# Weights of 48 columns, receptances scaled from PSUM, rows by ScalarE, deeper loads and two units ahead of a branch, in an RWKV attention with balanced experts

## The chip, the cores and the metric

One core of one Trainium2 chip. The metric is the device time of one execution in microseconds (us); quoted times are medians of the runs of one kernel, with lowest and highest. A profile is of one execution; its span is some 2 us less than that execution's time.

## The reference

```python
def attention(r, k, v, w, u):                  # r, k, v: (4, 8, 768, 48)
    state = zeros(B, H, D, D)
    for t in range(S):
        cur = outer(u * k[t], v[t])
        y[t] = r[t] @ (state + cur)
        state = w[:, None] * state + outer(k[t], v[t])     # w in 0.85..0.95

def experts(x, w_gate, w1, w2):                # x: (3072, 384), 8 experts, F = 1024
    # tokens are given to experts greedily by logit, 384 to each
    for e in range(8):
        out[mask[e]] = relu(x[mask[e]] @ w1[e]) @ w2[e]
```

All of it is float32. The output of the attention, (batch, position, head and column), is x.

## The kernel before

The attention is cut into 24 units (4 batches, 6 chunks of 128 positions). Within a chunk k is divided and r multiplied by powers of w, so that the pairs of positions are plain matmuls; this holds only if all w lie in a range, so a flag read at run time chooses between two arms of a branch, `attention_mild` (taken here) and `attention_any`. What is made ahead of the branch lies in the constructor of a class, the units in the arm. This is the constructor's loading, and one unit (HP is 4 pairs of heads, T 128 positions, D 48 columns of a head, DX all 384; tiles named _ps lie in PSUM, into which the matmuls write, the others in SBUF; `bufs` is the number of slots that a tile's name gets in a pool):

```python
self.lpool = ctx.enter_context(tc.tile_pool(name="m_load", bufs=5))       # ahead of the branch
...
for n in range(1, 3):
    self.load(n)            # a tile of lpool for k, one for r; v has fixed tiles
...
self.holds = nc.values_load(flag[0:1, 0:1])                               # the branch
...
def scale(n):                                                             # in the arm
    load(n + 3)
    kt, rt, vt = loaded.pop(n)
    ks, rs = kss[n % 4], rss[n % 2]
    nc.vector.tensor_mul(ks[:, :, 0:D], heads(kt), heads(wk))
    nc.vector.tensor_mul(rs[:, :, 0:D], heads(rt), heads(wr))
    rk = pool.tile([128, DX], F32, name="rk")
    nc.gpsimd.tensor_mul(rk, rt, kt)
    nc.gpsimd.tensor_mul(rk, rk, u_bc)
    dd = pool.tile([128, H], F32, name="dd")
    nc.vector.tensor_reduce(out=dd, in_=heads(rk), axis=AX.X, op=ALU.add)
    AT = pool.tile([128, 2, HP, T], F32, name="AT", bufs=3)
    for h in range(H):                                    # a diagonal for each head
        nc.scalar.activation(AT[:, h % 2, h // 2, :], ident, AF.Copy, scale=dd[:, h:h + 1])
def turn(n):
    ...                                                   # transposes of ks and rs
    kT = pool.tile([128, HP, T], F32, name="kT")          # bufs=2
    nc.scalar.copy(kT, kT_ps)
    rT = pool.tile([128, HP, T], F32, name="rT", bufs=3)
    nc.scalar.copy(rT, rT_ps)
def pairs(n):
    ...                                                   # g_ps = kT x rT, per head
    nc.vector.copy_predicated(out=AT[:, q], mask=..., data=g_ps[:, q])
def outputs(n):
    ...                                                   # y_ps = state x rT + vt x AT
    xT = pool.tile([128, HP, T], F32, name="xT", bufs=6)
    nc.scalar.copy(xT, y_ps)                              # frees y_ps, one buffer
    ...                                                   # kv_ps = ks x vt, to the state
for n in range(N):
    scale(n + 2); turn(n + 1); pairs(n + 1); outputs(n); rows(n - 1)   # shortened
```

The order of instructions on each engine is not that of the source: the compiler deals it from a model of the times, and puts a wait in front of an instruction where it reads or overwrites what another engine has not finished.

## Time and profile before

| | before |
|---|---|
| time, us | 474.58 (473.85 to 474.7), 3 runs |
| start, to g_ps of unit 0 | 23.6 us |
| 24 units | 133.7 us |
| assignment | 22.7 us |
| experts | 288.7 us |

The two views below are of the kernel before: first the waits in the units (engine, line and tile waiting; what for; us in all, times, the longest), then ScalarE's part of the timeline (start, duration, engine, line, operation, tiles, count, and in brackets the idle time ahead of it and what ended it).

```profile
ACT xT L492 <- PE y_ps L489: 34.2, 13, 3.8
```

### The profile page before, as it was taken

The numbers are of one execution on the slowest core, as the hardware profiler recorded it, in microseconds if no ns is written. First come the engines' busy times: TensorE is split into PE (matmuls) and PEld (weight loads), VectorE is DVE, ScalarE is ACT, GpSimd is POOL, SyncE is SP. The second block draws the span as 40 slices with busy tenths as digits, with TensorE's granted clock in tenths as the row PEclk, the third lists the DMA queues.
The fourth block names the chain that finished last, engine by engine and source line by source line (L and its number), as shares of the span: only waits on it lengthen the run. The fifth ranks groups of instructions, "written<-read, shape, count | busy, mean of one in ns | idle before, by whom it ended". The sixth has DMA issues, their size and how long they took to land. (4 is left out here: it accounts for less than half of the span.)

```text
span 468.7 us, 7836 instructions
## 1 busy us (share of the span) xinstructions
PE 409.7 (87%) x2900; PEld 276.4 (59%) x2900; DVE 217.5 (46%) x702; ACT 153.5 (33%) x390; POOL 123.5 (26%) x166
## 2 busy tenths in 40 slices
PE   0499999999999411999999999999999999999994
PEld 0387888889888300556556556556556556556552
DVE  5668878899984475440470460460550630300000
ACT  3668666667674000221221121211211211212200
POOL 2734474556560002021103012012021021301001
PEclk9999999999999855699999999999999999999998
DMA  9747555766631106253017027036035048601000
GB/s 156 114 96 162 125 129 120 156 147 141 139 84 36 58 1 242 79 211 127 34 42 298 31 78 277 18 105 250 17 138 216 17 172 317 203 0 38 13 17 34
DMA packets 93959, 54.36 MB, mean 116 GB/s; under 512 B 77137, under 2 KB 88530, under 8 KB 93906
## 3 DMA queue, kind: packets, MB, share of 16 engines
q1 hardware_dynamic: 89858, 44.05, 34.4%
q0 software_dynamic: 3072, 9.44, 5.5%
q8 instruction: 27, 0.44, 0.4%
q10 hardware_dynamic: 976, 0.21, 0.4%
q14 instruction: 26, 0.21, 0.2%
HBM read 44.25 MB, written 9.44 MB: 115 GB/s over the span
## 5 line engine op out<-in xcount | busy, mean ns | idle before, releaser
L1074 PE MATMUL h_ps<-xT,w 128*128 128x384 f32 x384 | 136.8, 504 | 1.4 <-ACT xT L1066 0.5
L1081 PE MATMUL o_ps<-w,hid 128*128 128x384 f32 x384 | 127.5, 486 | 0.0
L1081 PEld LDWEIGHTS o_ps<-w,hid 128*128 128x128 f32 x384 | 71.9, 190 | 47.2
L1074 PEld LDWEIGHTS h_ps<-xT,w 128*128 128x128 f32 x384 | 69.1, 193 | 45.5 <-issue 10.0
L1075 ACT ACTIVATE hid<-h_ps 128x384 f32<-128x384 f32 x64 | 31.4, 491 | 109.2 <-PE h_ps L1074 107.5
L1055 POOL DMA_INDIRECT xg<-x_rows,tok x24 | 23.3, 970 | 150.1 <-PE h_ps L1074 63.9
L444 ACT ACTIVATE AT<-ident,dd 128x128 f32<-128x128 f32 x192 | 58.8, 392 | 2.4 <-DVE dd L441 2.4
L1084 POOL DMA_INDIRECT out_dram<-o_sb,tok x24 | 23.7, 987 | 127.7 <-ACT o_sb L1083 122.5
L718 DVE TENSOR_TENSOR own<-counts,same 128x64 f32<-128x64 f32 x21 | 4.7, 225 | 102.0 <-PE counts L730 102.0
L1083 ACT COPY o_sb<-o_ps 128x384 f32<-128x384 f32 x24 | 11.5, 479 | 108.3 <-PE o_ps L1081 87.9
L438 POOL TENSOR_TENSOR rk<-rt,kt 128x384 f32<-128x384 f32 x24 | 26.2, 1095 | 41.7 <-DMA rt<-in_r_dram 38.6
L469 PE MATMUL g_ps<-rT,kT 48*128 48x128 f32 x384 | 28.8, 291 | 8.7 <-ACT rT L459 6.5
L472 DVE COPY_PREDICATED AT<-mask,g_ps 128x512 f32<-128x512 uint8 x48 | 32.2, 723 | 6.2 <-PE g_ps L469 6.1
L469 PEld LDWEIGHTS g_ps<-rT,kT 48*128 48x128 f32 x384 | 24.2, 193 | 12.7 <-ACT rT L459 10.2
L489 PE MATMUL y_ps<-AT,vt 128*64 128x128 f32 x384 | 29.7, 275 | 0.2 <-issue 0.2
L439 POOL TENSOR_TENSOR rk<-rk,u_bc 128x384 f32<-128x384 f32 x24 | 26.1, 1089 | 1.6
L492 ACT COPY xT<-y_ps 128x512 f32<-128x512 f32 x24 | 14.1, 586 | 36.9 <-PE y_ps L489 34.2
L485 PE MATMUL y_ps<-rT,state 128*64 128x128 f32 x320 | 25.7, 282 | 0.0
L489 PEld LDWEIGHTS y_ps<-AT,vt 128*64 128x64 f32 x384 | 24.6, 137 | 1.3 <-issue 0.4
L435 DVE TENSOR_TENSOR rs<-rt,wr 128x384 f32<-128x384 f32 x24 | 23.9, 996 | 0.7 <-ACT wr L361 0.2
L1066 ACT COPY xT<-xT_ps 128x384 f32<-128x384 f32 x24 | 10.9, 486 | 35.6 <-PE counts L730 32.0
L507 POOL TENSOR_TENSOR state<-state,wp 64x192 f32<-64x192 f32 x32 | 18.7, 584 | 11.2 <-DVE state L506 10.0
(170 smaller groups left out, 431.0 us busy)
## 6 DMA issues: line engine op xcount, KB each, us to landing
w<-in_moe_w_dram SPq DMA_DIRECT2D x16, 1536.0 KB, 8.0
kt<-in_k_dram SPq DMA_DIRECT2D x24, 192.0 KB, 3.6
rt<-in_r_dram SPq DMA_DIRECT2D x24, 192.0 KB, 3.3
vt<-in_v_dram SPq DMA_DIRECT2D x24, 192.0 KB, 3.6
x_rows<-xt SPq DMA_DIRECT2D x24, 192.0 KB, 2.3
xg<-x_rows,tok POOLq DMA_INDIRECT x24, 6.3
out_dram<-o_sb,tok POOLq DMA_INDIRECT x24, 2.6
u_bc<-in_u_dram ACTq DMA_DIRECT2D x1, 192.0 KB, 3.7
```

The source lines that it names most:

```text
L435: nc.vector.tensor_mul(rs[:, :, 0:D], heads(rt), heads(wr))
L438: nc.gpsimd.tensor_mul(rk, rt, kt)
L439: marks["rk"] = nc.gpsimd.tensor_mul(rk, rk, u_bc).ins
L444: nc.scalar.activation(AT[:, h % 2, h // 2, :], ident, AF.Copy, scale=dd[:, h:h + 1])
L469: g = nc.tensor.matmul(g_ps[:, q, a, :], kT[rows, a, :], rT[rows, a, :], start=True, stop=True)
L472: marks["AT"] = nc.vector.copy_predicated(out=AT[:, q], mask=mask.unsqueeze(1).to_broadcast([128, HP, T]), data=g_ps[:, q]).ins
L485: nc.tensor.matmul(y_ps[halves[q], a, :], S0[:, a, q, :], rT[:, a, :], start=(a == 0), stop=False, skip_group_check=True)
L489: nc.tensor.matmul(y_ps[halves[q], a, :], vt[:, 2 * a + q, :], AT[:, q, a, :], start=(c == 0 and a == 0), stop=(a == HP - 1), skip_group_c ...
L1074: nc.tensor.matmul(h_ps, w1[:, f, ts(j, 128)], xT[:, f, :], start=(f == 0), stop=(f == KD - 1))
L1075: nc.scalar.activation(hid[:, j, :], h_ps, AF.Relu)
L1081: nc.tensor.matmul(o_ps, hid[:, j, ts(c, 128)], w2[:, j, :], start=(j == 0), stop=(j == KF - 1))
L1084: nc.gpsimd.indirect_dma_start(out=out_rows[n * NC + c], out_offset=bass.IndirectOffsetOnAxis(ap=tok[:, c:c + 1], axis=0), in_=o_sb, in_of ...
```

## The change

Its intent: less for TensorE to load, a scaled copy of r saved, work moved off VectorE, and the first two units made while the flag is still on its way. The core of the diff, with cuts:

```diff
+        self.pool = ctx.enter_context(tc.tile_pool(name="m_work", bufs=2))     # ahead of the branch
-        self.lpool = ctx.enter_context(tc.tile_pool(name="m_load", bufs=5))
...                     # the transfer of w stands first; rt gets fixed tiles
+            (... for n in (("vt", 8), ("rt", 6), ("ks", 4)))
-        for n in range(1, 3):
+        for n in range(1, 4):
             self.load(n)
...
+            self.scale(0)
+            self.turn(0, ps)
+            self.scale(1)                                # still ahead of the branch
...
+        kt = self.pool.tile([128, H, D], F32, name="kt", bufs=6)
...                     # scale and turn become methods, with tiles of self.pool
+        AT = pool.tile([128, 2, H // 2, T], F32, name="AT", bufs=3)
+        rT = pool.tile([128, HP, T], F32, name="rT", bufs=3)
+        nc.vector.tensor_mul(rT, rT_ps, self.wr)
+        kT = pool.tile([128, HP, T], F32, name="kT")
+        nc.scalar.copy(kT, kT_ps)
...
-                nc.tensor.matmul(y_ps[halves[q], a, :], vt[:, 2 * a + q, :], AT[:, q, a, :],
+                nc.tensor.matmul(y_ps[halves[q], a, :], vt[:, 2 * a + q, 0:D], AT[:, q, a, :],
...                     # 48 columns for state and ks likewise; y_ps zeroed once
-        nc.vector.tensor_copy(heads(xt), xr_ps...)
+        nc.scalar.copy(xt..., xr_ps...)
...
-    scale(0)
-    scale(1)
-    turn(0)
     pairs(0)
```

More of the change, by code (lines that the diff above doesn't have):

```diff
@@ L24, with attention_any @@
 W_MIN, W_MAX = 0.7, 1.2
-def attention_any(ctx, tc, r, k, v, w, u, wg, x_dram, LG, ident, walk):
+def attention_any(ctx, kpads, rpads, tc, r, k, v, w, u, wg, x_dram, LG, ident, walk):
     nc = tc.nc
@@ L48, in attention_any @@
     ps_y = ctx.enter_context(tc.tile_pool(name="a_ps_y", bufs=1, space=PSUM))
-    NB = 3
-    kpads = [const.tile([128, H, PD], F32, name=f"kpad{i}") for i in range(NB)]
-    rpads = [const.tile([128, H, PD], F32, name=f"rpad{i}") for i in range(NB)]
+    NB = len(kpads)
     for i in range(NB):
@@ L293, in __init__ @@
         L = M + 1
-        self.tc, self.sources = tc, (k, r, v)
+        self.tc, self.r, self.k, self.v, self.ident = tc, r, k, v, ident
         const = self.const = ctx.enter_context(tc.tile_pool(name="m_const", bufs=1))
-        self.lpool = ctx.enter_context(tc.tile_pool(name="m_load", bufs=5))
+        self.pool = ctx.enter_context(tc.tile_pool(name="m_work", bufs=2))
         self.units = [(b, c) for c in range(C) for b in range(B)]
-        self.loaded = {}
-        self.vts, self.kss, self.rss = (
-            [const.tile([128, H, PD], F32, name=f"{name}{i}") for i in range(n)]
-            for name, n in (("vt", 6), ("ks", 4), ("rs", 2)))
-        for t in self.vts + self.kss + self.rss:
-            nc.vector.memset(t[:, :, D:PD], 0.0)
-        mask = const.tile([128, 128], F32, name="mask_f")
-        make_upper_triangular(nc, mask, val=1.0, diag=False)
-        self.mask = const.tile([128, 128], U8, name="mask")
-        nc.gpsimd.tensor_copy(self.mask, mask)
-        self.state = [const.tile([128, HP, 2, PD], F32, name=f"state{b}") for b in range(B)]
-        for t in self.state:
-            nc.scalar.activation(t.rearrange("p a q d -> p a (q d)"),
-                                 ident.unsqueeze(1).to_broadcast([128, HP, 128]), AF.Copy, scale=0.0)
-        self.wg_sb = const.tile([128, HP, 32], F32, name="wg_sb")
-        nc.vector.memset(self.wg_sb, 0.0)
+        self.loaded, self.live, self.marks = {}, {}, {}
         flat = w.rearrange("h d -> (h d)")
+        row = const.tile([1, DX], F32, name="row")
         wp = const.tile([P2, 8, HP], F32, name="wp")
@@ L321, in __init__ @@
                 nc.scalar.dma_start(wp[q * PD:q * PD + D, 0, :], w.rearrange("(a q) d -> q d a", q=2)[q])
-        row = const.tile([1, DX], F32, name="row")
         nc.sync.dma_start(row, flat.unsqueeze(0))
+        self.vts, self.rts, self.kss = (
+            [const.tile([128, H, PD], F32, name=f"{name}{i}") for i in range(n)]
+            for name, n in (("vt", 8), ("rt", 6), ("ks", 4)))
+        for i in range(8):
+            for t in (self.rts, self.vts, self.kss):
+                if i < len(t):
+                    (nc.vector if i < 2 else nc.gpsimd).memset(t[i][:, :, D:PD], 0.0)
+        self.wg_sb = const.tile([128, HP, 32], F32, name="wg_sb")
+        nc.vector.memset(self.wg_sb, 0.0)
         self.u_bc = const.tile([128, DX], F32, name="u_bc")
@@ L326, in __init__ @@
         nc.scalar.dma_start(self.u_bc, u.rearrange("h d -> (h d)").partition_broadcast(128))
+        for n in range(1, 4):
+            self.load(n)
         for q in range(2):
@@ L329, in __init__ @@
                                 wg.rearrange("(a q d) e -> q d a e", q=2, d=D)[q])
-        for n in range(1, 3):
-            self.load(n)
         up = const.tile([P2, HP, M + 2], F32, name="up")
@@ L350, in __init__ @@
         nc.vector.reciprocal(ch[:, :, L:T + 2], up[:, :, 1:M + 2])
-        turned = const.tile([P2, HP, T], F32, name="turned")
-        nc.scalar.copy(turned, ch[:, :, T + 1:1:-1])
-        self.wp, self.scales = wp, []
-        with tc.tile_pool(name="m_ps", bufs=2, space=PSUM) as ps, ExitStack() as part:
-            for name, t in (("wk", ch), ("wr", turned)):
-                sc_ps = ps.tile([128, HP, P2], F32, name="sc_ps")
-                for a in range(HP):
-                    nc.tensor.transpose(sc_ps[:, a, :], t[:, a, 0:T], ident[0:P2, 0:P2])
-                sc = const.tile([128, DX], F32, name=name)
-                nc.scalar.copy(sc.rearrange("p (h d) -> p h d", h=H),
-                               sc_ps.rearrange("p a (q d) -> p (a q) d", q=2)[:, :, 0:D])
-                self.scales.append(sc)
+        self.wr = const.tile([P2, HP, T], F32, name="wr")
+        nc.scalar.copy(self.wr, ch[:, :, T + 1:1:-1])
+        self.wp = wp
+        mask = const.tile([128, 128], F32, name="mask_f")
+        make_upper_triangular(nc, mask, val=1.0, diag=False)
+        self.mask = const.tile([128, 128], U8, name="mask")
+        nc.gpsimd.tensor_copy(self.mask, mask)
+        self.state = [const.tile([128, HP, 2, PD], F32, name=f"state{b}") for b in range(B)]
+        for t in self.state:
+            nc.scalar.activation(t.rearrange("p a q d -> p a (q d)"),
+                                 ident.unsqueeze(1).to_broadcast([128, HP, 128]), AF.Copy, scale=0.0)
+        with tc.tile_pool(name="m_ps", bufs=1, space=PSUM) as ps, ExitStack() as part:
+            sc_ps = ps.tile([128, HP, P2], F32, name="sc_ps")
+            for a in range(HP):
+                nc.tensor.transpose(sc_ps[:, a, :], ch[:, a, 0:T], ident)
+            self.wk = const.tile([128, DX], F32, name="wk")
+            nc.scalar.copy(self.wk.rearrange("p (h d) -> p h d", h=H),
+                           sc_ps.rearrange("p a (q d) -> p (a q) d", q=2)[:, :, 0:D])
+            self.scale(0)
+            self.turn(0, ps)
+            self.scale(1)
             pool = part.enter_context(tc.tile_pool(name="mild", bufs=1))
@@ L377, in load @@
         b, c = self.units[n]
-        tiles = []
-        for name, src in zip(("kt", "rt", "vt"), self.sources):
-            H, D = src.shape[1], src.shape[3]
-            if name == "vt":
-                t = self.vts[n % len(self.vts)]
-                into = t[:, :, 0:D]
-            else:
-                t = self.lpool.tile([128, H * D], F32, name=name)
-                into = t.rearrange("p (h d) -> p h d", h=H)
-            self.tc.nc.sync.dma_start(into, src[b, :, ts(c, T), :].rearrange("h s d -> s h d"))
-            tiles.append(t)
@@ L389, in load, with scale @@
-        self.loaded[n] = tiles
+        H, D = self.r.shape[1], self.r.shape[3]
+        kt = self.pool.tile([128, H, D], F32, name="kt", bufs=6)
+        rt, vt = (ts_[n % len(ts_)] for ts_ in (self.rts, self.vts))
+        for src, into in ((self.k, kt), (self.r, rt[:, :, 0:D]), (self.v, vt[:, :, 0:D])):
+            self.tc.nc.sync.dma_start(into, src[b, :, ts(c, T), :].rearrange("h s d -> s h d"))
+        self.loaded[n] = kt, rt, vt
+    def scale(self, n):
+        nc, pool = self.tc.nc, self.pool
+        H, D = self.r.shape[1], self.r.shape[3]
+        self.load(n + 4)
+        kt, rt, vt = self.loaded.pop(n)
+        ks = self.kss[n % len(self.kss)]
+        nc.vector.tensor_mul(ks[:, :, 0:D], kt, self.wk.rearrange("p (h d) -> p h d", h=H))
+        rk = pool.tile([128, H, D], F32, name="rk")
+        nc.gpsimd.tensor_mul(rk, rt[:, :, 0:D], kt)
+        self.marks["rk"] = nc.gpsimd.tensor_mul(rk, rk, self.u_bc.rearrange("p (h d) -> p h d", h=H)).ins
+        dd = pool.tile([128, H], F32, name="dd")
+        nc.vector.tensor_reduce(out=dd, in_=rk, axis=AX.X, op=ALU.add)
+        AT = pool.tile([128, 2, H // 2, T], F32, name="AT", bufs=3)
+        for h in range(H):
+            nc.scalar.activation(AT[:, h % 2, h // 2, :], self.ident, AF.Copy, scale=dd[:, h:h + 1])
+        self.live[n] = dict(vt=vt, ks=ks, rt=rt, AT=AT)
@@ new lines, in turn @@
+    def turn(self, n, ps):
+        nc, pool = self.tc.nc, self.pool
+        HP = self.r.shape[1] // 2
+        ks, rt = self.live[n]["ks"], self.live[n].pop("rt")
+        rT_ps = ps.tile([128, HP, T], F32, name="rT_ps")
+        for a in range(HP):
+            nc.tensor.transpose(rT_ps[:, a, :], rt[:, 2 * a:2 * a + 2, :].rearrange("p q d -> p (q d)"), self.ident)
+        kT_ps = ps.tile([128, HP, T], F32, name="kT_ps")
+        for a in range(HP):
+            nc.tensor.transpose(kT_ps[:, a, :], ks[:, 2 * a:2 * a + 2, :].rearrange("p q d -> p (q d)"), self.ident)
+        rT = pool.tile([128, HP, T], F32, name="rT", bufs=3)
+        nc.vector.tensor_mul(rT, rT_ps, self.wr)
+        kT = pool.tile([128, HP, T], F32, name="kT")
+        nc.scalar.copy(kT, kT_ps)
+        self.live[n].update(kT=kT, rT=rT)
@@ L410, in attention_mild @@
     E = wg.shape[1]
-    const = ctx.enter_context(tc.tile_pool(name="a_const", bufs=1))
     pool = ctx.enter_context(tc.tile_pool(name="a_work", bufs=2))
     ps = ctx.enter_context(tc.tile_pool(name="a_ps", bufs=1, space=PSUM))
-    units, load, loaded = mild.units, mild.load, mild.loaded
-    u_bc, wg_sb, wp = mild.u_bc, mild.wg_sb, mild.wp
-    wk, wr = mild.scales
-    halves = [slice(q * PD, q * PD + PD) for q in range(2)]
-    kss, rss, mask, state = mild.kss, mild.rss, mild.mask, mild.state
-    live, turned, marks = {}, {}, {}
-    def heads(t):
-        return t.rearrange("p (h d) -> p h d", h=H)
-    def pair(t, a):
-        return t[:, 2 * a:2 * a + 2, :].rearrange("p q d -> p (q d)")
-    def scale(n):
-        load(n + 3)
-        kt, rt, vt = loaded.pop(n)
-        ks, rs = kss[n % 4], rss[n % 2]
-        nc.vector.tensor_mul(ks[:, :, 0:D], heads(kt), heads(wk))
-        nc.vector.tensor_mul(rs[:, :, 0:D], heads(rt), heads(wr))
-        rk = pool.tile([128, DX], F32, name="rk")
-        nc.gpsimd.tensor_mul(rk, rt, kt)
-        marks["rk"] = nc.gpsimd.tensor_mul(rk, rk, u_bc).ins
-        dd = pool.tile([128, H], F32, name="dd")
-        nc.vector.tensor_reduce(out=dd, in_=heads(rk), axis=AX.X, op=ALU.add)
-        AT = pool.tile([128, 2, HP, T], F32, name="AT", bufs=3)
-        for h in range(H):
-            nc.scalar.activation(AT[:, h % 2, h // 2, :], ident, AF.Copy, scale=dd[:, h:h + 1])
-        live[n] = dict(vt=vt, ks=ks, rs=rs, AT=AT)
-    def turn(n):
-        ks, rs = live[n]["ks"], live[n]["rs"]
-        kT_ps = ps.tile([128, HP, T], F32, name="kT_ps")
-        for a in range(HP):
-            nc.tensor.transpose(kT_ps[:, a, :], pair(ks, a), ident)
-        rT_ps = ps.tile([128, HP, T], F32, name="rT_ps")
-        for a in range(HP):
-            nc.tensor.transpose(rT_ps[:, a, :], pair(rs, a), ident)
-        kT = pool.tile([128, HP, T], F32, name="kT")
-        nc.scalar.copy(kT, kT_ps)
-        rT = pool.tile([128, HP, T], F32, name="rT", bufs=3)
-        nc.scalar.copy(rT, rT_ps)
-        live[n].update(kT=kT, rT=rT)
+    units, live, marks = mild.units, mild.live, mild.marks
+    wg_sb, wp, mask, state = mild.wg_sb, mild.wp, mild.mask, mild.state
+    halves = [slice(q * PD, q * PD + D) for q in range(2)]
+    y_ps = ps.tile([128, HP, T], F32, name="y_ps")
+    nc.vector.memset(y_ps, 0.0)
+    turned = {}
     def pairs(n):
@@ L467, in pairs @@
             for q in range(2):
-                rows = slice(q * PD, q * PD + D)
-                g = nc.tensor.matmul(g_ps[:, q, a, :], kT[rows, a, :], rT[rows, a, :], start=True, stop=True)
+                g = nc.tensor.matmul(g_ps[:, q, a, :], kT[halves[q], a, :], rT[halves[q], a, :], start=True, stop=True)
         live[n].update(g=g.ins)
@@ L480, in outputs @@
         S0 = state[b]
-        y_ps = ps.tile([128, HP, T], F32, name="y_ps")
         if c > 0:
@@ L484, in outputs @@
                 for q in range(2):
-                    nc.tensor.matmul(y_ps[halves[q], a, :], S0[:, a, q, :], rT[:, a, :],
+                    nc.tensor.matmul(y_ps[halves[q], a, :], S0[:, a, q, 0:D], rT[:, a, :],
                                      start=(a == 0), stop=False, skip_group_check=True)
@@ L499, in outputs @@
                     for q in range(2):
-                        nc.tensor.matmul(kv_ps[halves[q], a, :], ks[:, 2 * a + q, :], vt[:, 2 * a + q, 0:D],
+                        nc.tensor.matmul(kv_ps[halves[q], a, :], ks[:, 2 * a + q, 0:D], vt[:, 2 * a + q, 0:D],
                                          start=True, stop=True)
@@ L503, in outputs @@
                 own = S0[halves[q], :, q, 0:D]
-                wc = wp[halves[q], 7, :].unsqueeze(2).to_broadcast([PD, HP, D])
+                wc = wp[halves[q], 7, :].unsqueeze(2).to_broadcast([D, HP, D])
                 if c > 0:
@@ L517, in rows @@
         xt = pool.tile([128, DX], F32, name="xt", bufs=3)
-        nc.vector.tensor_copy(heads(xt), xr_ps.rearrange("p a (q d) -> p (a q) d", q=2)[:, :, 0:D])
+        nc.scalar.copy(xt.rearrange("p (h d) -> p h d", h=H),
+                       xr_ps.rearrange("p a (q d) -> p (a q) d", q=2)[:, :, 0:D])
         nc.sync.dma_start(x_dram[ts(b * C + c, 128), :], xt)
@@ L541, in attention_mild @@
         if n + 2 < N:
-            scale(n + 2)
+            mild.scale(n + 2)
         if n + 1 < N:
-            turn(n + 1)
+            mild.turn(n + 1, ps)
             pairs(n + 1)
@@ L1027, in rwkv5_eagle_then_base_layer_balanced @@
             with ExitStack() as arm:
-                attention_any(arm, *arguments)
+                attention_any(arm, mild.kss[0:3], mild.rts[0:3], *arguments)
     walk.open(ctx)
```

## The prediction

> **What bounds the kernel now.** I read the stretches first, to know which part the change can reach at all.
>
> ```profile
> core 0: us, PE busy (x) PEld busy (x) DVE busy (x) ACT busy (x) POOL busy (x), PEclk, DMA share, GB/s
> 23.60:157.30 133.70, 130.82 (x1884) 114.12 (x1884) 104.86 (x211) 89.48 (x252) 64.17 (x94) 1.00 0.54 120
> 157.30:180.00 22.70, 2.96 (x24) 1.56 (x25) 15.87 (x73) 0.00 (x0) 0.00 (x0) 0.60 0.05 14
> 180.00:468.70 288.70, 270.95 (x972) 156.86 (x971) 81.78 (x376) 53.07 (x112) 46.96 (x48) 0.97 0.34 121
> ```
>
> The program is a start of 23.6 us, the 24 attention units in 133.7 us (5.57 each), an assignment of 22.7 us on VectorE, and the experts, 288.7 us. The diff touches the first two stretches: 157.3 us of the 468.7 us span. In the units TensorE is busy for 130.8 of 133.7 us; VectorE (104.9) and ScalarE (89.5) have room. So the units are TensorE's, if its busy time is real work; and the start is a chain. The start, from the timeline:
>
> ```profile
> 3.17 0.95 ACTq L321 DMA_DIRECT2D wp<-in_w_dram  x2
> 7.39 0.17 DVE L337 TENSOR_SCALAR wp<-wp 128x4 f32<-128x4 f32 x1 [3.20 <-DMA wp<-in_w_dram]
> 9.66 1.78 DVE L350 RECIPROCAL ch<-up 128x260 f32<-128x260 f32 x1
> 13.56 0.48 ACT L361 COPY wr<-sc_ps 128x384 f32<-128x384 f32 x1 [0.37 <-PE sc_ps L359]
> 14.26 2.50 POOL L438 TENSOR_TENSOR rk<-rt,kt 128x384 f32<-128x384 f32 x2 [2.93 <-ACTq L372]
> 18.33 4.78 ACT L444 ACTIVATE AT<-ident,dd 128x128 f32<-128x128 f32 x16 [2.43 <-DVE dd L441]
> 23.02 0.56 ACT L459 COPY rT<-rT_ps 128x512 f32<-128x512 f32 x1
> 23.63 2.08 PE L469 MATMUL g_ps<-rT,kT 48*128 48x128 f32 x16 [6.49 <-ACT rT L459]
> ```
>
> Column one is the start in us, two the time, the bracket what ended the idle time. The decays w are asked for only at 3.17 and land at 7.3; their powers end at 11.44 (9.66 + 1.78). POOL's first product waits until 14.26 for ScalarE to read the branch flag. ScalarE then makes the diagonals of two units (4.78 us) before it copies the first turned receptances, and TensorE, which transposed them by 16.1, stands 6.5 us. Last, what TensorE does in one unit, and the waits inside the units:
>
> ```profile
> 81.38 1.09 PE L485 MATMUL y_ps<-rT,state 128*64 128x128 f32 x16
> 82.30 1.04 PE L489 MATMUL y_ps<-AT,vt 128*64 128x128 f32 x16
> 83.17 0.38 PE L500 MATMUL kv_ps<-vt,ks 128*64 128x48 f32 x6
> 83.51 1.16 PE L469 MATMUL g_ps<-rT,kT 48*128 48x128 f32 x16
> ...
> 85.08 0.66 PE L516 MATMUL xr_ps<-ident,xT 128*128 128x128 f32 x4
> 85.57 0.60 PE L452 MATMUL kT_ps<-ident,ks 128*128 128x128 f32 x4
> 86.01 0.60 PE L455 MATMUL rT_ps<-ident,rs 128*128 128x128 f32 x4
> ```
>
> ```profile
> POOL rk L438 <- DMA rt<-in_r_dram: 38.6, 17, 7.4
> DVE dd L441 <- POOL rk L439: 9.0, 7, 2.1
> PE g_ps L469 <- DVE AT L472: 2.2, 3, 1.1
> ```
>
> Start to start, four transposes take 0.44 us, 16 y_ps matmuls 0.92 and 0.87, g_ps 1.09 (84.60 is the next start), kv_ps about 0.8, xr_ps 0.49. With the 0.53 us between the rT_ps transposes and the next y_ps a unit is 5.15 us, and a quarter of the gate's 1.0 us makes 5.4. The tenth rows start lies at 89.57 by the store of x, the nineteenth at 139.0: 5.5 us per unit. So TensorE has nearly no slack, and its real stalls are the three waits for copy_predicated, 1.1 + 1.35 + 0.5 us start to start: about 3 us. Their root is the first line: receptances land just before use, POOL's product is late, the reduction dd waits for it in VectorE's order, and the copy_predicated behind dd keeps the g_ps bank.
>
> **What the skill says.** "TensorE: Matmul & The Clock Gate", section "LDWEIGHTS (loading the stationary operand)": the time goes with the weight's columns (P / 1.2 ns), not its rows. The trace agrees in direction: a load of 32 columns takes 109 ns, of 64 137, of 128 in g_ps 193, so 0.875 ns a column, and 48 should take some 123. "SBUF — State Buffer", section "Who interferes with whom": a VectorE instruction with two SBUF inputs contends with a GpSimd one that reads SBUF, one with a single SBUF input doesn't. It agrees: rs<-rt,wr has a mean of 996 ns but 550 where POOL is idle, while the PSUM reads stay at 557 and 723. "VectorE: DVE Perf Modes", section "Why PSUM operands drop a tier": f32 from PSUM runs at one element a cycle, and its table gives 0.96 GHz; the copy of 384 from PSUM at 557 ns is 400 + 157. "TensorE: Matmul & The Clock Gate", section "What's actually happening": the array falls to half clock after idleness. The trace has it: 16 g_ps take 2.08 us at 23.63 and 1.16 later.
>
> **The change, part by part.**
>
> Weights of 48 columns. It touches y_ps from state (320), y_ps from AT (384) and kv_ps (320). What sets the step of y_ps? A transpose loads 128 columns and streams 128 rows in 109 ns (0.44/4). Two y_ps matmuls, on the two halves of the array, load 64 each and stream 128 rows in 109 (0.87/8). The same step at half the width: the streamed rows set it, the load is hidden, and 48 columns give nothing: 0. kv_ps streams only 48 rows: by the same rate 41 ns, while its step in pairs is about 58, near the 56 that 64 columns take at 0.875 ns. There the load binds; 48 columns make it 42 to 45. I take 13 ns off 8 pairs of 20 units: 2.1 us, say 2.
>
> Receptances scaled from PSUM. VectorE loses rs, 24 x 996 ns = 23.9 us. It gains a product of 512 from PSUM: 157 + 533 = 690 ns, 24 of them 16.6 us. ScalarE loses the rT copy, 24 x 584 ns = 14.0 us. The transposes need no scaled input any more, and the second scale (four transposes and a copy at the start) falls away.
>
> Rows of x by ScalarE. VectorE loses 24 x 557 = 13.4 us; ScalarE gains 24 x 0.48 (the wk copy has that shape) = 11.5. Together VectorE goes down by 20.7 us, ScalarE by 2.5, TensorE not at all. As the units are TensorE's, 0.86 us of VectorE per unit only lets g_ps's bank come free earlier: part of the 3 us.
>
> Loads deeper. One unit further ahead, 6 buffers of k and r for 5, 8 of v for 6: the first wait line should nearly vanish and with it the chain to copy_predicated. With the part before: 2 to 3 of the 3 us. I take 2.5. The bytes are the same, and the 0.54 DMA share leaves room.
>
> Two units ahead of the branch. This is where I expect most. The w transfer stands first, so it should go out at about 1 and land at about 4.3 (3.2 to 4.1 us as measured) rather than 7.3: 3 us earlier. The powers take 4.05 us as before: 8.4. The ch transposes (1.1 us, cold) and the wk copy end at about 10.2, ks(0) at 10.8, kT(0)'s four transposes at 11.9, its copy at 12.5. Receptances of unit 0 are transposed raw before that, and their product by VectorE waits for no ScalarE queue. POOL's products run before the branch, so that the diagonals of unit 0 (2.45 us of ScalarE) lie at about 9 to 14, possibly ahead of the kT copy. So g_ps of unit 0 starts at 12.5 to 14.5, 13.5 in the middle, against 23.63: 10.1 us. I give back 1.5 us: at 23.6 the old kernel had four units scaled on VectorE and POOL, the new one has two, and TensorE will wait for unit 1's diagonals and copy (2.45 + 0.58 us on ScalarE). Net 8.6.
>
> Sum: 8.6 + 2 + 2.5 = 13.1 us; the tail (0.48 for 0.56 us of the last copy of x) adds less than 0.1. From 474.6: 461.5. The order of TensorE's instructions will be dealt anew, and each change between kinds of matmul costs some 0.1 us (a group's first step is 160 to 200 ns for 109), so I round to 462.
>
> **The rivals.** First: the weight load is on the path for y_ps too. Then 1024 loads lose 14 ns each; over two halves that is 7.2 us, over one 14.3, and the time would be 457 or less. For it: load time of 114 us in the units. Against: the equal step at 128, 64 and 32 columns (the gate does 32 in 1.0 us, four to a step). Second: the start gains little, because the flag is read by ScalarE only after the diagonals of both units, and whatever waits for the branch, POOL above all (2.93 us today), waits longer; or because DMA binds: five units land from 3 to 18.5 us, about 3.1 us each, at a mean share of 1 there, and the deeper loads add a sixth. For it: these waits. Against: unit 0 lands by 6.5 and unit 1 by 9.5, well before TensorE's need. If it held, the start would give 4 and the time would be 467. Third: ScalarE becomes the bound, since its order now has kT, xT, rows and diagonals one behind another, and a late rows copy holds back the next kT. Per unit it stays 4.2 us of 5.4; against it. It would cost the stall gains: 465. Fourth: the product of receptances now stands between transposes and g_ps in VectorE's order, behind a waiting dd; if loads still came late, TensorE would stall at each unit and the gain at the start would be eaten: 470.
>
> **Range and chances.** Centre 462. The start may give 5 to 11, the units 0 to 8: 456.5 to 468.5. Over 2% faster is below 465.1; it fails if the start gives half or the new order loses some us: 0.76 for faster, 0.22 for the same, 0.02 for slower, as work falls on every engine.
>
> **What would show it.** g_ps should start at 12.5 to 14.5 us; the end of the units should come near 144. The y_ps groups should keep 0.87 to 0.92 us for 16, with loads of 123 ns; kv_ps should fall from about 0.8 to 0.65. The wait of rk for rt should be under 10 us, and g_ps should not wait for copy_predicated. The product of receptances should be near 690 ns, the rows copy on ScalarE 480. Experts and assignment should stay as they are. I am wrong if y_ps's step falls, if g_ps starts after 18, or if a unit in the middle takes over 5.6 us.

## More of the kernel before

```profile
79.57 0.59 ACT L492 COPY xT<-y_ps 128x512 f32<-128x512 f32 x1 [2.76 <-PE y_ps L489]
80.06 2.45 ACT L444 ACTIVATE AT<-ident,dd 128x128 f32<-128x128 f32 x8
...
82.41 0.57 ACT L457 COPY kT<-kT_ps 128x512 f32<-128x512 f32 x1
82.87 0.58 ACT L459 COPY rT<-rT_ps 128x512 f32<-128x512 f32 x1
83.39 0.59 ACT L492 COPY xT<-y_ps 128x512 f32<-128x512 f32 x1
```

ScalarE waits for y_ps only to copy it (xT); the diagonals AT follow without a wait, since they go to a buffer that is long free.

## The result, and the profile after

| | before | after |
|---|---|---|
| time, us | 474.22 (472.56 to 474.7), 4 runs | 489.73 (488.75 to 490.1), 4 runs |
| ratio | | 1.033, 95% interval 1.030 to 1.036: slower |
| g_ps of unit 0 starts, us | 23.63 | 17.36 |
| 24 units, us | 133.7 | 157.6 |
| assignment and experts, us | 311.4 | 313.5 |

The start came 6.3 us earlier and the units take 23.9 us longer; the rest is as it was but for 2 us. (The stretches differ by 19.7 us in all and the times by 15.5: the profiled execution of the kernel before took 470.84 us, less than its four timed runs.) By stretches, the changed kernel (columns: the stretch in us, its length, then busy time and instructions of each engine, granted clock of TensorE, share of DMA, GB/s):

```profile
17.30:174.90 157.60, 142.40 (x1888) 114.29 (x1888) 91.10 (x193) 88.69 (x260) 61.65 (x95) 0.99 0.46 103
174.90:199.00 24.10, 3.06 (x25) 1.55 (x25) 15.80 (x72) 0.48 (x1) 0.00 (x0) 0.58 0.07 16
199.00:488.40 289.40, 271.66 (x972) 157.23 (x971) 81.99 (x376) 53.07 (x112) 47.04 (x48) 0.97 0.34 120
```

No engine has more to do: VectorE went from 104.9 to 91.1 us in the units, ScalarE from 89.5 to 88.7. TensorE's busy time reads 142.4 for 130.8, but its matmuls are as many (1888 and 1884 recorded) and nearly as long (those of y_ps from AT 281 ns in the mean, 275 before): their records overlap, and here they overlap less, so this is not more work. Beyond that TensorE is idle for 15 us of 157.6, where it was idle for 3 of 133.7. So the units stand in waits. The waits of the changed kernel in this stretch:

```profile
ACT AT L404 <- PE y_ps L479: 59.2, 21, 3.7
POOL rk L398 <- DVE dd L401: 38.8, 12, 4.8
DVE AT L463 <- ACT AT L404: 17.8, 8, 5.1
...
PE y_ps L475 <- ACT xT L482: 13.6, 16, 2.2
```

The first line is new: the diagonals of nearly each unit wait for a y_ps matmul, 2.8 us each time. One unit in the middle, of the timeline of the changed kernel:

```profile
110.16 1.05 PE L475 MATMUL y_ps<-rT,state 128*48 128x128 f32 x14 [0.66 <-ACT xT L482]
...
111.14 1.16 PE L460 MATMUL g_ps<-rT,kT 48*128 48x128 f32 x16
...
112.38 1.14 PE L479 MATMUL y_ps<-AT,vt 128*48 128x128 f32 x15
...
113.56 2.45 ACT L404 ACTIVATE AT<-ident,dd 128x128 f32<-128x128 f32 x8 [2.69 <-PE y_ps L479]
...
115.75 1.34 DVE L463 COPY_PREDICATED AT<-mask,g_ps 128x512 f32<-128x512 uint8 x2
115.92 0.56 ACT L482 COPY xT<-y_ps 128x512 f32<-128x512 f32 x1
...
116.62 1.05 PE L475 MATMUL y_ps<-rT,state 128*48 128x128 f32 x14 [0.66 <-ACT xT L482]
```

This is a closed ring. TensorE computes y_ps of a unit (110.16 to 113.5). Only when the last y_ps matmul has read AT does ScalarE begin the next AT (113.56). The copy xT stands behind these eight diagonals (115.92), and only it frees the one buffer of y_ps, so that the next unit's y_ps begins at 116.62. The period is 3.40 to the diagonals, 2.36 to the copy and 0.70 to the next y_ps: 6.46 us, for 5.5 in the kernel before, in which the diagonals took no part. A second arm runs beside it: copy_predicated writes into the same AT and waits for the diagonals too (17.8 us in the list), here from 115.75 to 117.09. No run takes the two arms apart; both hang on the one buffer of AT.

Why would AT have to wait for the unit just before, with three buffers? The compiled programs give the addresses of the buffers, in bytes of a partition, in the order of use:

```text
              made ahead of the branch    made behind it, in turn
before   AT   -                           87104 95296 91200 87104 95296 91200 ...
         kT   -                           99392 101440 99392 101440 ...
         kt   68608 74752 73216           71680 70144 71680 70144 ...
         rt   76288 82432 80896           79360 77824 79360 77824 ...
after    AT   91712 99904                 95808 95808 95808 95808 ...
         kT   110144                      112192 112192 112192 ...
         kt   79360 87040 85504 ... (6)   79360 87040 79360 87040 ...
```

In these programs a tile made ahead of the branch and still in use behind it keeps its slot throughout the arm; the two slots of kt that do rotate after the change are those of units 0 and 1, which are read to the end ahead of the branch. The change makes AT of units 0 and 1 ahead of the branch, so of three buffers one is left for the other 22 units; of kT's two one is left, and of kt's six two (four hold the units loaded ahead). The kernel before has the same on a small scale: of its five buffers of k and r, three were loaded ahead, and two rotate.

### The profile page after: what moved, and what is told of

It is laid out like the page before. It is cut to its first block, busy times and chain, and to the rows that moved or that the text cites. A ratio compares the mean times of both kernels' runs of the same rounds, so it can differ in the third digit from the quotient of the medians.

```text
span 488.4 us, 7858 instructions
## 1 busy us (share of the span) xinstructions
PE 420.4 (86%) x2896; PEld 275.2 (56%) x2896; DVE 199.7 (41%) x673; ACT 149.7 (31%) x389; POOL 120.3 (25%) x178
## 5 line engine op out<-in xcount | busy, mean ns | idle before, releaser
L475 PE MATMUL y_ps<-rT,state 128*48 128x128 f32 x320 | 31.0, 287 | 13.6 <-ACT xT L482 13.6
L398 POOL TENSOR_TENSOR rk<-rt,kt 128x384 f32<-128x384 f32 x24 | 24.8, 1033 | 66.7 <-DVE dd L401 38.8
L463 DVE COPY_PREDICATED AT<-mask,g_ps 128x512 f32<-128x512 uint8 x48 | 32.3, 725 | 19.4 <-ACT AT L404 17.8
L479 PE MATMUL y_ps<-AT,vt 128*48 128x128 f32 x384 | 32.8, 281 | 0.0
L475 PEld LDWEIGHTS y_ps<-rT,state 128*48 128x48 f32 x320 | 20.0, 126 | 20.9 <-issue 13.8
L479 PEld LDWEIGHTS y_ps<-AT,vt 128*48 128x48 f32 x384 | 25.1, 126 | 1.4 <-ACT xt L508 0.4
L395 DVE TENSOR_TENSOR ks<-kt,wk 128x384 f32<-128x384 f32 x24 | 18.1, 762 | 13.6 <-PE kv_ps L490 13.5
L414 PE MATMUL rT_ps<-ident,rt 128*128 128x128 f32 x96 | 16.7, 297 | 6.3 <-DMA rt<-in_r_dram 6.3
```

What stands on the lines that cost most here:

```text
L398: nc.gpsimd.tensor_mul(rk, rt[:, :, 0:D], kt)
L463: marks["AT"] = nc.vector.copy_predicated(out=AT[:, q], mask=mask.unsqueeze(1).to_broadcast([128, HP, T]), data=g_ps[:, q]).ins
L475: nc.tensor.matmul(y_ps[halves[q], a, :], S0[:, a, q, 0:D], rT[:, a, :], start=(a == 0), stop=False, skip_group_check=True)
L479: nc.tensor.matmul(y_ps[halves[q], a, :], vt[:, 2 * a + q, 0:D], AT[:, q, a, :], start=(c == 0 and a == 0), stop=(a == HP - 1), skip_group ...
```

## The experiments

Theory: the one rotating buffer of AT costs the units some 24 us. Rivals, from the prediction: ScalarE's order with the rows of x in it; VectorE's order with the product of receptances in it; weight loads. The first four ran together; on that chip the kernel before took 471.77 us (470.35 to 472.96, 7 runs). Ratios are against the kernel before on the same chip.

**AT in three fixed tiles that rotate by hand, nothing else.**

```diff
+        self.ATs = [const.tile([128, 2, HP, T], F32, name=f"AT{i}") for i in range(3)]
-        AT = pool.tile([128, 2, H // 2, T], F32, name="AT", bufs=3)
+        AT = self.ATs[n % 3]
```

> The changed kernel with the three diagonal buffers AT as fixed tiles used in turn (unit n takes n modulo 3) in place of a pool of three. No memory is added. Theory (the two diagonals made ahead of the branch hold two of the pool's three buffers through the whole branch, so that each unit's diagonals wait for the y of the unit before, and ScalarE makes them before it copies that y out): a unit falls from 6.45 to 5.3 to 5.6 us, TensorE's wait for the copy of y goes, and the time is 458 to 467 us. Rival (ScalarE is too full since it copies the rows of x, or the receptance product in VectorE's order holds g_ps): the time stays over 483 us.

Measured: 465.81 us (464.67 to 467.68, 4 runs), ratio 0.988 (0.984 to 0.992). The same number of bytes, with the slots handed out by hand, is worth 24 us by the medians (489.73 to 465.81) and 21 by the two ratios, since the kernel before was 2.45 us faster in these rounds. It turns a slower kernel into one that is 1.2% faster than the kernel before. By stretches the units took 133.2 us again, for 157.6:

```profile
17.80:151.00 133.20, 128.16 (x1888) 111.45 (x1888) 93.05 (x193) 90.87 (x261) 63.08 (x94) 1.00 0.53 119
```

Each edit has the order dealt anew, but two other edits below (one buffer in the kernel before; units 0 and 1 behind the branch) lead to the same cause, and together they settle it. But the units are only as fast as before the change, so the gains predicted within them are still missing. The waits of this run in the units begin with these:

```profile
POOL rk L399 <- DMA kt<-in_k_dram: 28.7, 12, 5.2
ACT AT L405 <- PE y_ps L480: 28.2, 21, 3.2
```

The second line is the wait blamed above, at half its sum. With three slots in turn ScalarE still waits there, but it no longer reaches TensorE: its wait for xT (13.6 us, 16 times, in the changed kernel) is not in this run's list at all. POOL's wait for k is the next candidate.

**The kernel before with one buffer of AT.**

```diff
-        AT = pool.tile([128, 2, HP, T], F32, name="AT", bufs=3)
+        AT = pool.tile([128, 2, HP, T], F32, name="AT", bufs=1)
```

> The kernel before with one diagonal buffer AT in place of three, nothing else. Theory: that alone makes the slowdown: the units go from 5.5 to 6.3 to 6.7 us and the time to 490 to 502 us (474 plus 21 units by 0.8 to 1.2 us and no gain at the start). Rivals: one buffer is enough when nothing else changes, 474 to 479 us.

Measured: 507.5 us (503.24 to 508.56, 4 runs), ratio 1.074 (1.067 to 1.080). The direction is the theory's: one buffer is enough to slow the units, without anything else of the change. The size is beyond what was expected. The waits of the diagonals for y_ps are 72.0 us in its units, and the granted clock fell in the first part of them, which the changed kernel's (0.99) did not:

```profile
21.10:100.00 78.90, 70.07 (x795) 55.92 (x795) 45.01 (x109) 38.39 (x110) 30.34 (x54) 0.85 0.45 97
100.00:194.00 94.00, 83.76 (x1092) 67.79 (x1090) 51.96 (x107) 52.59 (x152) 31.44 (x42) 0.98 0.38 88
```

So TensorE also worked slower for part of the time. How much of the excess is the clock, and how much the order, which was dealt anew, no run separates.

**The changed kernel with rows of x by VectorE.**

```diff
-        nc.scalar.copy(xt..., xr_ps...)
+        nc.vector.tensor_copy(xt..., xr_ps...)
```

> The changed kernel with the rows of x copied by VectorE again, as before. Theory of the pinned buffers: the rows copy comes after the copy of y in ScalarE's order and is not in the loop, so 486 to 491 us. Rival (ScalarE too full): 470 to 479 us.

Measured: 489.78 us (489.2 to 490.61, 4 runs), ratio 1.039 (1.035 to 1.042). A hit for the theory: ScalarE's rows are not what costs the 24 us. (They come back below.)

**The changed kernel with units 0 and 1 made behind the branch.**

```diff
-            self.scale(0); self.turn(0, ps); self.scale(1)      # ahead of the branch
+    mild.scale(0); mild.turn(0, ps); mild.scale(1)              # first in the arm
     pairs(0)
```

> The changed kernel with the scaling and turning of the first two units moved behind the branch again, all other parts kept. Theory: no diagonal is held over the branch, the three buffers rotate, a unit takes 5.3 to 5.6 us, and the start loses a part of what it had won: 466 to 473 us. Rivals that blame another part: it stays over 483 us.

Measured: 467.34 us (466.97 to 467.98, 4 runs), ratio 0.990 (0.987 to 0.994). A hit: the pools are those of the changed kernel, untouched; it is enough that AT, kT and rT are made behind the branch. The compiled program of this run has AT at 91712, 99904 and 95808 in turn, and ScalarE waits for y_ps only to copy it (37.1 us), as in the kernel before. g_ps of unit 0 starts at 20.7 us here, so nearly half of the gain at the start (23.6 to 17.4) does not come from the two units but from the rest of what the change does there.

The next four ran on the same chip; the kernel before took 471.66 us (470.35 to 472.96, 8 runs).

**All four rings: AT, kT, rT and kt rotate by hand (3, 2, 3 and 6 tiles).**

```diff
+        self.kTs, self.rTs, self.kts = ...          # 2, 3 and 6 fixed tiles
-        kt = self.pool.tile([128, H, D], F32, name="kt", bufs=6)
+        kt = self.kts[n % 6]                        # rT and kT alike, AT as above
```

> The changed kernel with AT, kT, rT and kt all as fixed tiles that rotate by hand (3, 2, 3 and 6 of them, the counts of the changed kernel). With AT alone rotating, the run before gave 465.8 us, and its units took no less than those of the kernel before; there POOL's product still waited 28.7 us for k, and the g_ps matmuls stood about 5.1 us behind copy_predicated. Theory: the pinned buffers of k (two of six rotate) cause these, so the wait for k goes under 5 us, the stalls of g_ps nearly vanish, and the time is 460 to 463. Rival: k comes late because the DMA engines have no more to give, or because VectorE stands in the way; then it stays at 464.5 to 467 and the wait moves to r or to VectorE.

Measured: 463.35 us (461.88 to 465.1, 5 runs), ratio 0.981 (0.978 to 0.984). 2.5 us less than with AT alone, with intervals that just touch; just beyond the 460 to 463 of the theory, below the 464.5 of the rival. POOL's wait for k is gone from the list. But the stalls of g_ps did not vanish. The largest, of this run's timeline:

```profile
47.15 0.18 DVE L689 TENSOR_SCALAR rel<-digits 128x16 f32<-128x16 int32 x1 [1.92 <-POOL digits L665]
...
48.48 0.68 DVE L423 TENSOR_TENSOR rT<-rT_ps,wr 128x512 f32<-128x512 f32 x1
...
49.31 1.16 PE L464 MATMUL g_ps<-rT,kT 48*128 48x128 f32 x16 [1.65 <-DVE rT L423]
```

VectorE has to do, among the units, small constants for the assignment later. It waits 1.92 us for POOL to make one, and the receptances of the next unit, which TensorE needs, stand behind it in VectorE's order. The prediction's fourth rival is this, with another wait in the place of dd.

**The last power of w ahead of POOL's products.**

```diff
+            self.marks["ch"] = ... .ins             # of the last of POOL's powers, as written
+        with tc.issue_after(self.marks["ch"]):      # queued behind it, for units 0 and 1
             nc.gpsimd.tensor_mul(rk, rt[:, :, 0:D], kt)
```

> All four rings rotate, and POOL's products rk of units 0 and 1 are queued behind the last power of ch. In the changed kernel g_ps of unit 0 starts at 17.4 us since three products of 1.0 us stand between POOL's powers; the powers should then end near 9 instead of 12.6 and g_ps start at 13.5 to 15. Theory (the start is a chain, TensorE's units follow it): 2 to 3.5 us less than with the rings alone. Rival: the diagonals of units 0 and 1, made later on ScalarE, take it back: within 1 us of the rings alone.

Measured: 462.63 us (462.15 to 462.94, 5 runs), ratio 0.981. A miss of mine: the power written last is tiny and depends on none of the long ones, so the compiler had put it early, and POOL's order did not change (its powers ended at 12.75 us as before). The run is a second measurement of the four rings and tells nothing of the start.

**64 columns again.**

```diff
-                nc.tensor.matmul(y_ps[...], vt[:, 2 * a + q, 0:D], AT[:, q, a, :], ...)
+                nc.tensor.matmul(y_ps[...], vt[:, 2 * a + q, :], AT[:, q, a, :], ...)
                 # state and ks alike
```

> All four rings rotate, and the weights of y_ps and kv_ps have 64 columns again (zeros taken along), as in the kernel before. If the step of kv_ps alone depends on the columns, as the starts in the two traces say (38 ns against 25 in the mean, 320 of them): 2 to 4 us more than with 48 columns. If the loads bind y_ps too (the first rival of the prediction): 7 us or more. If the shorter steps only end earlier in front of another wait: within 1 us.

Measured: 463.62 us (462.46 to 465.9, 6 runs), ratio 0.983 (0.980 to 0.987), the four rings 0.981. Within 1 us: beside these waits no gain of 48 columns is seen.

**Four rings, rows of x by VectorE.**

```diff
             # the four rings, and
-        nc.scalar.copy(xt..., xr_ps...)
+        nc.vector.tensor_copy(xt..., xr_ps...)
```

> All four rings rotate, and the rows of x are copied by VectorE again. If ScalarE's order (diagonals, turned outputs, rows) holds TensorE up once the buffers rotate, this is 1 to 3 us faster than rows on ScalarE; if VectorE's copy_predicated is what holds it up, 1 to 3 us slower; if neither, within 1 us.

Measured: 459.05 us (458.33 to 459.49, 5 runs), ratio 0.972 (0.970 to 0.975). 4.3 us less than with rows on ScalarE, more than expected, and the fastest kernel of this study: it beats both. By stretches TensorE has no idle time left in its units, and the list of waits has 0.7 us for it; VectorE took the rows on and has room:

```profile
17.70:146.60 128.90, 128.75 (x1888) 112.46 (x1888) 100.39 (x217) 81.15 (x237) 60.26 (x94) 1.00 0.54 123
```

The copy has not only moved, the orders were dealt anew with it, and the receptances of that unit now stand ahead of the wait:

```profile
46.09 0.67 DVE L423 TENSOR_TENSOR rT<-rT_ps,wr 128x512 f32<-128x512 f32 x1
...
47.73 0.22 DVE L689 TENSOR_SCALAR rel<-digits 128x16 f32<-128x16 int32 x1 [0.51 <-POOL digits L665]
```

So of the 4.3 us a part, up to 1.65 us at this one place of the profiled execution, is the dealt order of VectorE and not ScalarE's time; the runs don't separate the rest.

The last four ran on another chip; there the kernel before took 472.43 us (469.96 to 473.74, 11 runs), and comparisons with the runs above go by the ratios.

**The kernel before with fixed tiles for k and r, five each.**

```diff
-                t = self.lpool.tile([128, H * D], F32, name=name)
+                t = (self.kts if name == "kt" else self.rts)[n % 5]
```

> The kernel before, with its buffers of k and r (5 each) as fixed tiles that rotate by hand; nothing else. In the kernel before only two of the five rotate behind the branch. Theory (the late receptances of the kernel before come from that, and its three stalls of copy_predicated from them): the wait of POOL for r falls from 38.6 us to under 10, and the time falls by 2 to 3 us, the 2.5 us that the prediction put on deeper loads. Rival (the wait only moves to VectorE or to the diagonals' buffers): within 1 us.

Measured: 468.98 us (467.68 to 471.35, 6 runs), ratio 0.993 (0.990 to 0.997), 3.1 us by the ratio, a little more than the 2 to 3. In the profile POOL's wait for r (38.6 us before) is no longer there at all, and none of the three stalls of about 1 us of g_ps behind copy_predicated is left. So the prediction saw a real loss, but read its cause wrongly: the loads were not issued too few units ahead, their buffers did not rotate.

**POOL's powers ahead of its products in fact, rows by VectorE.**

```diff
+            if m == n:
+                self.marks["ch"] = p                # the last of the long powers
+                # rk of unit 1 behind rk of unit 0, dd of unit 1 behind ks of unit 0
```

> Four rings, rows of x on VectorE, and now in fact all of POOL's powers ahead of its products (the run before put them behind the last power as written, which is the smallest and not the last in POOL's order, so POOL's order stayed), products unit by unit, and VectorE scales k of units 0 and 1 before it waits for unit 1's product. Powers should end at 9.5 to 10.5 us in place of 12.7 and g_ps of unit 0 start at 15 to 16 in place of 17.8. If the start is one chain: 456 to 457.5, 1.5 to 3 us less than with POOL's order as dealt. Rival: POOL's products of units 0 to 3 end no earlier, and copy_predicated of unit 0 stands behind their reductions in VectorE's order, so TensorE waits a little later: within 1 us of 459.

Measured: 460.27 us (457.99 to 461.57, 6 runs), ratio 0.975 (0.972 to 0.979). The rival's result: the powers end at 9.8 us, g_ps of unit 0 starts 1.6 us earlier, and nothing comes of it. The timeline of this run says where it goes:

```profile
16.20 2.08 PE L473 MATMUL g_ps<-rT,kT 48*128 48x128 f32 x16 [0.72 <-ACT kT L434]
...
18.50 0.55 DVE L413 TENSOR_REDUCE dd<-rk 128x8 f32<-128x384 f32 x1 [0.90 <-POOL rk L408]
...
20.22 1.33 DVE L476 COPY_PREDICATED AT<-mask,g_ps 128x512 f32<-128x512 uint8 x2
...
21.00 0.45 PE L492 MATMUL y_ps<-AT,vt 128*48 128x128 f32 x1 [0.81 <-DVE AT L476]
```

g_ps is done at 18.3, but copy_predicated starts at 20.22, against 20.58 in the run with POOL's order as dealt: in VectorE's order it stands behind the reductions dd of later units, and these wait for POOL's products. The transposes of the last unit's rows start at 145.83 us in this profile and at 145.84 in the other.

**64 columns, rows by VectorE.**

```diff
             # the four rings, rows by VectorE, and
-                nc.tensor.matmul(y_ps[...], vt[:, 2 * a + q, 0:D], AT[:, q, a, :], ...)
+                nc.tensor.matmul(y_ps[...], vt[:, 2 * a + q, :], AT[:, q, a, :], ...)
                 # state and ks alike
```

> Four rings, rows of x on VectorE, weights of 64 columns. With rows on ScalarE, 48 columns gave nothing (463.4 for 463.6) though kv_ps's steps fell. Theory: there other waits took the 2 to 3 us, and here, where TensorE has nearly no waits left between 30 and 140 us, 64 columns cost 1.5 to 3 us: 460.5 to 462. Rival: the shorter steps of kv_ps are paid back in the change to the next kind of matmul, so they are worth nothing at all: within 1 us of 459.

Measured: 460.82 us (460.01 to 462.13, 6 runs), ratio 0.977 (0.974 to 0.980), against 0.972 with 48 columns: 0.4%, 1.9 us. The two intervals overlap by a little, so the times alone don't settle it; the profiles agree with it: from the start of g_ps of unit 0 to that of the last transposes of rows 129.5 us against 128.1, and this line of groups (busy us and mean ns), first with 64 and then with 48 columns:

```profile
L495 PE MATMUL kv_ps<-vt,ks 128*64 128x48 f32 x320 | 17.5, 226 | 0.0
```

```profile
L494 PE MATMUL kv_ps<-vt,ks 128*48 128x48 f32 x320 | 15.7, 214 | 0.0
```

With 48 columns kv_ps is 1.8 us shorter and y_ps (60.5 us of busy time for 60.6) is not: what remains of 48 columns is kv_ps, and only where TensorE is the bound.

**Four rings, rows by VectorE, units 0 and 1 behind the branch.**

```diff
             # the four rings, rows by VectorE, and
-            self.scale(0); self.turn(0, ps); self.scale(1)      # ahead of the branch
+    mild.scale(0); mild.turn(0, ps); mild.scale(1)              # first in the arm
```

> Four rings, rows of x on VectorE, and the scaling and turning of units 0 and 1 moved back behind the branch. g_ps of unit 0 should start at 20 to 21 us (20.7 in the run with everything in the arm) in place of 17.8. If all of that comes through to the end: 461.5 to 462.5, so that the two units ahead of the branch are worth 2.5 to 3.5 us. If TensorE then only waits for the buffers of later units either way: within 1 us of 459.

Measured: 463.02 us (462.14 to 464.06, 6 runs), ratio 0.982 (0.979 to 0.984), against 0.972: 0.9%, 4.3 us by the ratios, with intervals apart, and just beyond the 461.5 to 462.5 expected. g_ps of unit 0 starts at 20.5 us, 2.75 later, and the span of the profile is 2.6 us longer. So two units ahead of the branch are worth some 2.6 to 4.3 us once their tiles don't hold the arm's buffers, and this comes through to the end.

## Why the prediction was wrong

The prediction was 462 us, faster; the result was 489.73, slower by 3.3%.

**The step that failed** is the line under "Rows of x by ScalarE" and in the range, that the units stay TensorE's and "work falls on every engine", with the sum that adds the start, kv_ps and the stalls to an unchanged unit (the units were to give 0 to 8 us and cost 23.9). It took the buffer counts in the source (3 of AT, 2 of kT, 6 of k) for the counts that rotate. The part "Two units ahead of the branch", on which it counted most, was costed by time only; what it takes is slots. In place of an unchanged unit of 5.5 us the runs showed one of 6.5, by the ring of AT, y_ps and xT: 24 us, given back by rotating AT alone. Its test was the right one: "if a unit in the middle takes over 5.6 us".

The trace of the kernel before held the hint. "The wait of rk for rt", 38.6 us, was read as loads not deep enough; it was the same thing, three of five slots held by what was loaded ahead of the branch, as the run with five fixed tiles shows (3.1 us). The Trainium skill names this sign: "Perfetto Trace Analysis", section "Optimization Strategy", says that the same gap coming again and again, on the engine that should be full, can mean that the next tile finds no room, and names the buffer count. The changed kernel's trace agrees: TensorE waits for xT 16 times, 13.6 us in all, behind the 21 waits of the diagonals of 2.8 us each; only, the count in the source was enough, and two of its slots lay idle after the second unit.

**Start: too large.** Net 8.6 us was predicted, from g_ps at 12.5 to 14.5. It started at 17.36. The decays w, predicted to land at 4.3 us, were first used at 5.95, so VectorE's powers ended at 10.0 for 8.4. And in the changed kernel's timeline POOL's powers do not run as one chain of 4 us: products of the first two units, 1.0 us each, stand between them, and the receptances wait:

```profile
5.95 0.17 DVE L330 TENSOR_SCALAR wp<-wp 128x4 f32<-128x4 f32 x1 [1.25 <-DMA wp<-in_w_dram]
...
8.20 1.00 POOL L398 TENSOR_TENSOR rk<-rt,kt 128x384 f32<-128x384 f32 x1
...
9.76 1.00 POOL L399 TENSOR_TENSOR rk<-rk,u_bc 128x384 f32<-128x384 f32 x1
...
12.36 0.41 POOL L341 TENSOR_TENSOR ch<-ch,wp 128x128 f32<-128x128 f32 x1
...
12.80 0.62 ACT L346 COPY wr<-ch 128x512 f32<-128x512 f32 x1 [6.40 <-POOL ch L341]
```

But putting POOL's powers ahead brought no time, so behind this chain lies another, POOL's products to copy_predicated of unit 0, that the prediction did not have.

**kv_ps: right in mechanism and near in size** (2 predicted, about 1.9 measured, not settled by the intervals), where TensorE is the bound; not seen where it is not. **y_ps: right**, its weight loads went from 137 to 126 ns (123 predicted), its busy time was the same with 64 and with 48 columns (60.6 and 60.5 us), and 64 columns cost 1 to 2 us where the first rival asks for 7 or more, so it is out. The working's 0.875 ns a column is drawn through g_ps's loads and leaves out those of the transposes, 128 columns in 140 to 149 ns; between 32 and 64 columns it did for 48.

**Stalls, 2.5 us: right in size, wrong in cause**, as said; in the changed kernel as built it could not show.

**The rivals.** The second, a start that gains little, came half true (6.3 us of 10.1), but not by the wait for the flag, since POOL's products ran ahead of it; whether the loads made w late no run tells. The third, ScalarE's order costing the gains within the units ("465"), is what the kernel with rings does: 463.4 to 465.8 with rows on ScalarE, 459.05 without; but it is the dealt order as a whole that moved, and no run shows ScalarE itself full (91 of 133 us). The fourth is real at single places (1.65 us). The 4.3 us in which both may have a part are small against 24. The receptance product was 689 ns (690 predicted), the rows copy 473 (480), and assignment and experts stayed within 2 us.

Put together, with the slots rotating and rows on VectorE, the parts of the change give 12.6 us on the kernel before (471.66 to 459.05); the prediction's sum was 13.1, with other terms, so that this is no confirmation of it. (Its range is about 1 us narrower at each end than its parts give: 5 to 11 and 0 to 8 off 474.6 are 455.6 to 469.6.)

**What stays open:** what part of the excess with one buffer of AT in the kernel before is the clock; how the 4.3 us of the rows split between ScalarE's time and the dealt order. Higher counts in the pools instead of rings by hand could not be tried: with four or five buffers of AT the program does not build, since the pool of the other arm finds too little room.

## What to carry to other kernels

When work is moved ahead of a branch or a loop, count the buffers that are left to rotate behind it: a tile that lives across the boundary may hold its slot for all that follows, and one rotating buffer makes producer and consumer take turns. Look at the addresses in the compiled program, or for one wait that comes in each unit with the same length, and give such tiles fixed slots by index. And before a shorter step is counted as a gain, ask whether its engine is the bound in that stretch: 48 columns showed no gain beside other waits and about 2 us without them, which the times alone do not settle.

## What the Trainium skill lacked or had wrong

- None of its pages has that a tile made ahead of a branch and used behind it keeps its slot in the whole arm; here it cost 24 us of 490 (489.73 to 465.81 by rotating AT alone).
- "TensorE: Matmul & The Clock Gate", section "LDWEIGHTS (loading the stationary operand)": P / 1.2 ns gives 40 ns for 48 columns; the trace records 126 ns, and 137 for 64. The difference of 11 ns is near its slope (13), the recorded duration is not. Nor do these loads go by columns alone: 128 columns took 140 to 149 ns in the transposes and 193 in g_ps; no run here tells why. The gain at the clock is smaller still, 1.8 us of busy time over 320 matmuls, and only in kv_ps, which streams 48 columns.
